# Dense products in two halves of 64 rows, the lower half one tile behind

## The chip, the core and the metric

The kernel runs on one core of one Trainium2 chip. The metric is the device time of one execution in microseconds (us). TensorE multiplies matrices into PSUM, VectorE, ScalarE and GpSimd work on vectors, and SyncE, ScalarE and GpSimd issue transfers (DMAs). TensorE has one queue of instructions; a matmul in it is preceded by the load of its stationary operand (its weights). PSUM has eight banks of 512 columns.

## The reference

Attention with a compressive memory beside a gated feed-forward block, mixed by a gate. Cut to what matters:

```python
for s in range(N):                                   # 4 chunks of L = 512 rows, 32 heads of 20
    logits = einsum("bhqd,bhkd->bhqk", qs, ks) * scale + mask
    a_dot = einsum("bhqk,bhkd->bhqd", softmax(logits), vs)
    num = einsum("bhld,bhde->bhle", phi(qs), M)
    den = einsum("bhld,bhd->bhl", phi(qs), z)[..., None] + 1e-6
    outs.append(g * num / den + (1.0 - g) * a_dot)
    M, z = M + einsum("bhld,bhle->bhde", phi(ks), vs), z + phi(ks).sum(2)
a = concat(outs) @ wo                                # D = 640
b = (silu(x @ w1) * (x @ w3)) @ w2                   # F = 1728
out = sigmoid((x * gate_w).sum(-1)) * a + (1 - that) * b
```

## The kernel before, in words

Everything dense (q, k, v, the two up products g and u, the down product f, the output product op) is a product of 640 or 128 rows at a time, in three passes of high and low parts in single precision's fast form. A **tile** is one PSUM bank: 15 matmuls of 128 rows by 512 columns for q, k, g and u, 15 of 320 columns for v and op, and 9 (in one group 5) of 320 columns for f. After its last matmul an engine empties the bank: VectorE and ScalarE make `ft`, `fu`, `ht` from g and u, VectorE adds f and op into `acc`.

The attention works on **pairs** of heads `p`, two pairs to a **quad**. A head has 60 or 62 rows, so the two heads of a pair stand in rows 0 to 63 and 64 to 127, and the array is split into two halves of 64 rows for them. For each pair there are three `s_unit`s (logits of queries against keys; VectorE takes each row's maximum, line 626, with an instruction that reads the maximum out behind each) and three `t_unit`s (the logits once more, turned, with the maximum taken off; ScalarE makes the exponential `P`, GpSimd cuts it at the diagonal). `pv_quad` multiplies P by V with the array cut into four column strips, 16 matmuls (32 on the chip, since plain single precision takes two passes).

TensorE's order is written by the program itself; the other engines' order comes from a scheduler. The attention is a generator of 40 slots for each quad. In four of them, `VISITS` (slots 5, 15, 25, 35), it issues its units together, s and t units of 1408 columns per head, the first with `pv_quad` ahead. Between visits the dense work is drawn from `segs`, a queue of jobs, by a credit in nanoseconds. Before a visit the running tile is carried up to the next place where its bank is filled. `bank_tile` hands out the eight banks in turn.

Weights are loaded by `w_load` into `wraw`, and split into high and low parts by `w_split` into one of `NW` = 6 buffers; `clock["oldest"]` says which weights are still needed.

Of the kernel before, what the change touches and what calls it, by code (L numbers as in the profile page):

```python
# [17 lines left out]
P = 128  # L18
# [8 lines left out]
NST, NW, NRAW, NHT, NVG, NB = 4, 6, 2, 6, 2, 8  # L27
# [6 lines left out]
PSEG = ((0, 512), (512, 384), (1024, 256), (896, 128))  # L34


@with_exitstack
def gated_mix(ctx: ExitStack, tc: tile.TileContext, xT, wqk, wv, w13, w2, w2h, wo, beta, out):
# [19 lines left out]
    sel = cp.tile([96, D], BF, name="sel")  # L58
    rs = cp.tile([P, P], F32, name="rs")
    rp = cp.tile([P, 3, P], BF, name="rp")  # L60
    rR = cp.tile([96, L], BF, name="rR")
# [28 lines left out]
    def selection():  # L90

        here(nc.gpsimd.memset(sel, 1.0))
        nc.gpsimd.affine_select(sel[:32], sel[:32], pattern=[[1, D]], base=0, channel_multiplier=-DH,
                                compare_op=ALU.is_ge, fill=0.0)
        nc.gpsimd.affine_select(sel[:32], sel[:32], pattern=[[-1, D]], base=DH - 1, channel_multiplier=DH,
                                compare_op=ALU.is_ge, fill=0.0)
        for i in (32, 64):
            nc.gpsimd.tensor_copy(sel[i:i + 32], sel[:32])
# [19 lines left out]
    free, held = list(range(NB)), {}  # L118

    def bank_tile(name, hold=None):  # L120


        k = free.pop(0)
        ps = pp.tile([P, L], F32, tag=f"b{k}", name=name, bufs=1)
        if hold:
            held[k] = -hold
        else:
            free.append(k)
        return ps

    def filled():

        free.extend(held)
        held.clear()

    def split_psum(dst, src, name, pin=lambda ins: ins):

        hi = bank_tile(name)[:, :src.shape[-1]]
# [37 lines left out]
    def w_split():  # L176
        k, raw, n, _, after = raws.pop(0)
        w = sp.tile([P, 2, D + 2], FR, tag="W", name=f"W{k}", bufs=NW)
        tiles[k] = w
        split(w[:, :, :n], raw[:, :n], lo=nc.vector.tensor_sub if k < 7 else None, pin=behind(after))  # L180
# [17 lines left out]
    def w_get(i, oldest=None):  # L198
# [6 lines left out]
        clock["oldest"] = i if oldest is None else oldest  # L205
# [81 lines left out]
    def proj(ps, w, x):  # L287
        n = 0
        for kb in range(KB):
            for a, b in PASSES:  # L290
                nc.tensor.matmul(ps, w[:, a, kb * P:(kb + 1) * P], x[:, b, kb, :],  # L291
                                 start=n == 0, stop=n == 14)
                n += 1
            if kb < KB - 1:
                yield 699
        filled()
# [47 lines left out]

    def q_block(c, mb, i, alloc, oldest=None):
        ps = bank_tile(f"q{c}_{mb}", 1300)
        yield from proj(ps, w_get(i, oldest), Xs[c])
        if c:
            if mb == 0:
                big["q", c] = alloc(f"pq{c}")  # L350
        s = parts(f"qs{c}_{mb}", ps, big["q", c][:, mb * L:(mb + 1) * L] if c else None)
        store_parts(0, c, mb, s)
        yield 699

    def q_pair(c, i, j):

        ws = [w_get(i), w_get(j, i)]
        ps = [bank_tile(f"q{c}_{mb}") for mb in range(2)]
# [14 lines left out]
    def memory_read(c):  # L373
        pq = big.pop(("q", c))[:, :KB * L].rearrange("p (b n) -> p b n", b=KB)
        for qb in range(4):
            for hf in range(2):
                gm = f_tile(f"gm{c}_{qb}_{hf}")[:, :320]
                ps = bank_tile(f"nd{c}_{qb}_{hf}")
                nd = ps[:, :16 * VE].rearrange("p (h e) -> p h e", e=VE)
                todo = []  # L380
                for b in range(KB):
                    a0, a1 = HEADS[b]
                    u0, u1 = max(a0, 16 * hf), min(a1, 16 * hf + 15)
                    if u0 <= u1:
                        todo.append((b, a0, u0, u1))
                for n, (b, a0, u0, u1) in enumerate(todo):
                    nc.tensor.matmul(nd[:, u0 - 16 * hf:u1 - 16 * hf + 1, :],  # L387
                                     pq[:, b, qb * P:(qb + 1) * P],
                                     Ms[c - 1, b][:, u0 - a0:u1 - a0 + 1, :],
                                     start=n == 0, stop=n == len(todo) - 1, skip_group_check=True)  # L390
# [6 lines left out]
                store_later(gd[c][:, qb, 320 * hf:320 * hf + 320], gm, ("g", c, qb), n=2)  # L397
                yield 700

    def v_blocks(c, iv, end):  # L400
# [6 lines left out]
        wvt = [w_get(i, iv[0]) for i in iv]  # L407
        for lb in range(4):
            if keep:
                vv = V[:, lb]  # L410
            else:
                vv = ht_tile([P, H, VE], F32, f"vv{c}_{lb}")
                nc.gpsimd.memset(vv[:, :, DH:], 1.0)
            for hf in range(2):
                n0, n1 = (0, 320) if hf == 0 else (320, 642)
                ps = bank_tile(f"v{c}_{lb}_{hf}", 800)
                n = 0
                for kb in range(KB):
                    for a, b in PASSES:
                        nc.tensor.matmul(ps[:, :n1 - n0], x[:, a, kb, lb * P:(lb + 1) * P],  # L420
                                         wvt[kb][:, b, n0:n1], start=n == 0, stop=n == 14)
                        n += 1
                    if end and (lb, hf) == (3, 1):
# [635 lines left out]
```

## Time and profile before

| | |
|---|---|
| time, median of 3 (lowest to highest) | 1131.27 us (1130.45 to 1131.47) |
| profiled execution, first to last instruction (its own time is not listed apart) | 1129.4 us |
| TensorE busy, its matmuls | 1119.2 us (99%), 6952 |
| VectorE, GpSimd, ScalarE busy | 575.5 us, 545.1 us, 483.1 us |
| granted TensorE clock, mean | 0.998 |

The page's busy time of TensorE is the union of overlapping matmuls whose ends are modelled, so 99% does not say that the array streams without loss. In the timeline a line is a run of equal instructions: when the run begins, how long it lasts to the last one's end, engine, line, operation, output and inputs, count. The next run's start, not the first one's length, tells how long it kept the engine. PEld is the load of weights. In the groups, the two numbers behind the bar are busy time in us and the mean life of one in ns; behind the next bar stands the engine's idle time ahead of them.

### The profile page before, as it was taken

Reading aid. Unit: us, or ns where it says so; the run is one execution under the profiler, and the core shown is the slowest. Engines: PE = TensorE matmul, PEld = TensorE weight load, DVE = VectorE, ACT = ScalarE, POOL = GpSimd, SP = SyncE. Lnnn points to the kernel's source line nnn. Section 1 sums busy time; section 2 is a strip of 40 time slices with the busy share of each in tenths; the row PEclk is TensorE's granted clock in tenths of the full one; section 3 lists DMA queues with packets and bytes.
Section 4 is the critical chain, followed back from the end, with each engine's and each line's share of the span. In section 5 each row is a group of like instructions: output and inputs, shape, how many; then the busy total and the mean of one; then the engine's idle time right before and its main releaser. Section 6 shows DMA issues by size and latency. Waiting matters only on the chain.

```text
span 1129.4 us, 19596 instructions
## 1 busy us (share of the span) xinstructions
PE 1119.2 (99%) x6952; PEld 903.7 (80%) x6952; DVE 575.5 (51%) x1719; ACT 483.1 (43%) x988; POOL 545.1 (48%) x732
## 2 busy tenths in 40 slices
PE   9999999999999999999999999999999999999998
PEld 6988777877877888888977776788768778877988
DVE  6032564355655553565243667774546665651544
ACT  6255334544343242255355644535543444344040
POOL 5053356455455453455255446645764555465140
PEclk9999999999999999999999999999999999999999
DMA  8265753434344324435377864456643334342122
GB/s 313 95 233 204 234 128 93 97 88 114 77 113 104 96 65 120 140 83 179 107 244 247 266 214 134 101 135 166 174 120 106 91 95 110 88 133 76 48 59 94
DMA packets 85953, 152.01 MB, mean 135 GB/s; under 512 B 19936, under 2 KB 32992, under 8 KB 85856
## 3 DMA queue, kind: packets, MB, share of 16 engines
q1 hardware_dynamic: 55776, 94.48, 26.8%
q0 software_dynamic: 22880, 41.86, 15.4%
q10 hardware_dynamic: 7200, 14.42, 3.4%
q8 instruction: 55, 0.90, 0.3%
q14 instruction: 42, 0.34, 0.1%
HBM read 95.25 MB, written 54.53 MB: 133 GB/s over the span
## 4 chain that ended last, share of the span: by engine, by line
PE 93%; issue 2%; DMA 1%; DVE 1%; POOL 1%; ACT 1%; POOLq 0%; SPq 0%; ACTq 0%; DVEq 0%
PE g L291 17%; PE f L571 17%; PE u L291 16%; PE v L420 6%; PE o L670 6%; PE k L291 6%; PE q L291 6%; PE s L618 5%; PE op L813 4%; PE t L653 4%; PE pm L474 1%; PE nd L387 1%; PE q L366 1%; PE pkt L459 1%; PE gt L737 1%
## 5 line engine op out<-in xcount | busy, mean ns | idle before, releaser
L626 DVE CUSTOM_DVE_ANT_0 junk<-s,mask 128x128 bf16<-128x128 f32 (+3 forms) x512 | 251.1, 490 | 189.8 <-PE s L618 150.9
L116 POOL TENSOR_TENSOR W<-wr,W 128x640 fp32r<-128x640 f32 (+1 forms) x126 | 197.5, 1571 | 203.8 <-ACT W L115 160.7
L657 ACT ACTIVATE P<-t 128x384 f32<-128x384 f32 (+1 forms) x384 | 174.5, 533 | 165.2 <-PE t L653 164.2
L291 PE MATMUL g<-X,W 128*128 128x512 f32 x840 | 216.4, 401 | 0.0
L660 POOL TENSOR_SCALAR_AFFINE_SELECT P<-P 128x256 f32<-128x256 f32 (+1 forms) x192 | 94.2, 497 | 235.7 <-ACT P L657 235.2
L571 PE MATMUL f<-W,ht 128*128 128x320 f32 x1312 | 204.4, 313 | 1.0 <-ACT acc L577 0.7
L291 PE MATMUL u<-X,W 128*128 128x512 f32 x780 | 201.1, 401 | 0.0
L571 PEld LDWEIGHTS f<-W,ht 128*128 128x128 f32 x1312 | 194.3, 189 | 7.6 <-issue 3.3
L291 PEld LDWEIGHTS g<-X,W 128*128 128x128 f32 x840 | 153.5, 188 | 40.1 <-issue 5.7
L291 PEld LDWEIGHTS u<-X,W 128*128 128x128 f32 x780 | 143.1, 188 | 36.3 <-issue 3.8
L115 ACT CAST W<-wr 128x640 fp32r<-128x640 f32 (+1 forms) x131 | 94.2, 730 | 73.2 <-PE u L291 23.1
L642 POOL DMA_DIRECT2D qk<-mr x128 | 73.4, 576 | 49.4 <-DVE mr L637 40.2
L579 DVE SCALAR_TENSOR_TENSOR acc<-f,cgate,acc 128x320 f32<-128x320 f32 x128 | 69.5, 547 | 41.6 <-PE f L571 40.7
L116 POOL TENSOR_TENSOR ht<-ft,ht 128x512 fp32r<-128x512 f32 x52 | 67.2, 1292 | 46.3 <-ACT ht L115 46.1
L291 PE MATMUL k<-X,W 128*128 128x512 f32 x300 | 77.1, 403 | 0.0
L670 PE MATMUL o<-P,vg 128*32 128x512 f32 (+3 forms) x1024 | 75.7, 436 | 0.0
L813 PE MATMUL op<-W,oT 128*128 128x320 f32 x480 | 75.3, 313 | 0.0
L813 PEld LDWEIGHTS op<-W,oT 128*128 128x128 f32 x480 | 71.2, 189 | 2.5 <-issue 1.6
L420 PE MATMUL v<-W,X 128*128 128x320 f32 (+1 forms) x480 | 72.1, 311 | 0.6 <-DVE m L626 0.6
L420 PEld LDWEIGHTS v<-W,X 128*128 128x128 f32 x480 | 71.0, 189 | 1.5 <-PE q L291 1.0
L597 POOL DMA_DIRECT2D qk<-qkd x128 | 70.1, 552 | 0.0
L653 PE MATMUL t<-qk 62*128 62x256 f32 (+2 forms) x512 | 68.1, 338 | 0.6 <-DVE ns L141 0.3
(115 smaller groups left out, 1103.0 us busy)
## 6 DMA issues: line engine op xcount, KB each, us to landing
qk<-qkd POOLq DMA_DIRECT2D x128, 240.0 KB, 3.9
wr<-in_w_dram SPq DMA_DIRECT2D x80, 320.0 KB
qkd<-qs SPq DMA_DIRECT2D x20, 512.0 KB
qkd<-ks SPq DMA_DIRECT2D x20, 512.0 KB
od<-oq ACTq DMA_DIRECT2D x32, 256.0 KB
wr<-in_wo_dram SPq DMA_DIRECT2D x20, 320.0 KB
vg<-vd SPq DMA_DIRECT2D x16, 336.0 KB
xr<-in_xT_dram SPq DMA_DIRECT2D x20, 256.0 KB
```

Source lines behind the costliest of these rows:

```text
L115: pin(nc.scalar.copy(dst[:, 0], src))
L116: (lo or nc.gpsimd.tensor_sub)(dst[:, 1], src, dst[:, 0].bitcast(F32))
L291: nc.tensor.matmul(ps, w[:, a, kb * P:(kb + 1) * P], x[:, b, kb, :], start=n == 0, stop=n == 14)
L420: nc.tensor.matmul(ps[:, :n1 - n0], x[:, a, kb, lb * P:(lb + 1) * P], wvt[kb][:, b, n0:n1], start=n == 0, stop=n == 14)
L571: nc.tensor.matmul(ps[:, :320], a, b, start=n == 0, stop=n == len(ms) - 1)
L626: nc.vector.tensor_tensor_reduce(out=junk[:, :n], in0=ps[i][:, o:o + n], in1=mask[:, L - n:], scale=1.0, scalar=-3.0e38, op0=ALU.add, op1= ...
L642: after(4 + 9 * k, lambda d=dst, r=r: here(nc.gpsimd.dma_start(d, mr[r:r + 8])))
L653: nc.tensor.matmul(ps[i][:, o:o + L - q0], k[:, kb * P:(kb + 1) * P], q[:, q0:], start=kb != 2, stop=kb != 3, skip_group_check=True)
L657: last["exp"] = nc.scalar.activation(u["P"][:, i, o:o + n], ps[i][:, b:b + n], AF.Exp, scale=SCALE)
L660: nc.gpsimd.affine_select(d, d, pattern=[[0, 2], [0, n], [1, P]], base=0, channel_multiplier=-1, compare_op=ALU.is_ge, fill=0.0)
L670: nc.tensor.matmul(ps[32 * i:32 * i + 32, kb * P:], heads[2 * p + i]["v"][:, kb], pairs[p + i // 2]["P"][:, i % 2, o:o + n], start=kb == 0 ...
L813: nc.tensor.matmul(ps[:, :320], oT[0][:, qb % 2, a, kb * P:(kb + 1) * P], ws[kb][:, b, 320 * hf:320 * hf + 320], start=n == 0, stop=n == 14)
```

## The change

A dense product of 128 rows becomes two of 64 rows, in the upper and the lower half of the array, which add into the same bank. First all upper halves of a tile are issued, then all lower halves, and while a tile's lower halves run the next tile's upper halves do. `Work` is a tile, `under` the tile in the upper half, `behind_one` those that wait for the lower, `flight` the one in it. `put` keeps a clock for each half, and `step` issues for the half that is behind. The lower half of a tile begins when `APART` = 5 further upper matmuls have been issued, and behind a read by VectorE of one element of the bank (`seen`), which shows that the upper half is done.

The visits are gone: each s and t unit stands alone in a slot (`S_AT`, `T_AT`) amid dense products, which now have its shape. `pv_quad` moves to slot 2 of the quad after next's (from 5) and is what still changes the array's division. Transposes, the memory's products and the sums' spreading (`rr`, with a selection matrix rebuilt by GpSimd in the head) go in halves too. A bank is chosen by an expected time at which it comes free (`until`, `hold`). `NW` is 7, and side jobs are braided in by nanoseconds.

```diff
-NST, NW, NRAW, NHT, NVG, NB = 4, 6, 2, 6, 2, 8
+NST, NW, NRAW, NHT, NVG, NB = 4, 7, 2, 6, 2, 8
+COL, COL4, MIN_MM, APART = 0.4533, 1.667, 110, 5
...
-    def bank_tile(name, hold=None):
-        k = free.pop(0)
+    def bank_tile(name, hold=1500):
+        k = until.index(min(until))
+        until[k] = max(clocks) + hold
...
+    def halves(todo):
+        def half(f, r):
+            o, l, x, c = f() if callable(f) else f
+            return o, l[64 * r:64 * r + 64], x[64 * r:64 * r + 64], c, False
+        return tuple([lambda f=f, r=r: half(f, r) for f in todo] for r in range(2))
...
+    def one(r, w):
+        i, todo = w.at[r], w.todo[r]
+        o, l, x, c, turn = todo[i]() if callable(todo[i]) else todo[i]
+        if turn:
+            ins = nc.tensor.transpose(o, l, x)
+        else:
+            ins = nc.tensor.matmul(o, l, x, start=i == 0 and (r == 0 or not w.todo[0]),
+                             stop=i == len(todo) - 1 and (r == 1 or not w.todo[1]), skip_group_check=True)
+        if r == 0 and i == len(todo) - 1 and w.todo[1]:
+            nc.vector.tensor_copy(seen, w.ps[:1, :1])
+        dense["ns"] += put(r, c) / 2
...
+    def follow():
+        if flight[0] is None and behind_one and dense["n0"] >= behind_one[0].mark + APART:
+            flight[0] = w = behind_one.popleft()
...
-    def proj(ps, w, x):
-                nc.tensor.matmul(ps, w[:, a, kb * P:(kb + 1) * P], x[:, b, kb, :],
-                                 start=n == 0, stop=n == 14)
+    def proj(w, x):
+        def parts(ps):
+            return halves([(ps, w[:, a, kb * P:(kb + 1) * P], x[:, b, kb, :], L * COL) for kb in range(KB) for a, b in PASSES])
...
-        for i in (32, 64):
-            nc.gpsimd.tensor_copy(sel[i:i + 32], sel[:32])
+        for base, h0, n, f0, f1 in ((0, 0, R1H + 1, 0, R1B * P), (64, R1H, H - R1H, R1B * P, D)):
...
-    VISITS = {5: (((0, 0), (0, 1)), ((0, 0),)), 15: (((0, 2), (1, 0)), ((0, 1),)),
-              25: (((1, 1), (1, 2)), ((0, 2),)), 35: ((), ((1, 0), (1, 1), (1, 2)))}
+    S_AT = {3: (0, 0), 8: (0, 1), 11: (0, 2), 16: (1, 0), 19: (1, 1), 24: (1, 2)}
+    T_AT = {5: (0, 0), 13: (0, 1), 21: (0, 2), 27: (1, 0), 31: (1, 1), 35: (1, 2)}
```

On TensorE before, behind the quad `o12` in chunk 0's attention: the rest of a tile of g (chunk 0, hidden tile 7), the whole tile of u, six matmuls of the next g, then a visit (the second unit of the pairs 16 and 17, one unit t of pair 14), and g goes on. `X0` and `X1` are the chunks' inputs, `W35` and `W36` weights, `qk` the pairs' buffers; the last number in a name is the buffer's:

```order
L291 MATMUL g0_7_3441<-X0_102,W35_2924 128x512 x3
L291 MATMUL u0_7_3519<-X0_102,W36_3247 128x512 x15
L291 MATMUL g1_7_3544<-X1_104,W35_2924 128x512 x6
L618 MATMUL s16_2_0_3551<-qk0_86 128x512
L618 MATMUL s16_2_1_3552<-qk0_86 128x512
```

The same place on TensorE now, behind the same quad; each dense row is a half:

```order
L195 MATMUL g1_7_4947<-X1_105,W35_4082 128x512
L195 MATMUL g0_7_4832<-X0_103,W35_4082 128x512
L195 MATMUL g1_7_4947<-X1_105,W35_4082 128x512
L195 MATMUL g0_7_4832<-X0_103,W35_4082 128x512
L811 MATMUL s16_0_0_4976<-qk0_86 128x256
L811 MATMUL s16_0_1_4977<-qk0_86 128x256
L811 MATMUL s16_0_0_4976<-qk0_86 128x256
L811 MATMUL s16_0_1_4977<-qk0_86 128x256
L195 MATMUL g1_7_4947<-X1_105,W35_4082 128x512
L195 MATMUL g0_7_4832<-X0_103,W35_4082 128x512
```

Where a tile's 15 matmuls stood in a row, upper halves of g1 and lower halves of g0 now take turns, and the logits of a pair stand between two such rows.

On VectorE before, in the down product of chunk 0 (f0_6, hidden tiles 6 to 8): the maxima of a unit of pair 19 (`junk`, with `m` read out behind each), then the sums into `acc0`, one for each tile of f:

```order
L626 ISA junk_3832,m36_3639<-s19_0_1_3823,mask_85 128x128
L626 ISA m36_3639 128x1
L626 ISA junk_3834,m36_3639<-s19_0_1_3823,mask_85 128x256
L626 ISA m36_3639 128x1
L546 SCALAR_TENSOR_TENSOR ft1_8_3798<-fu1_8_3799,u1_8_3802 128x512
L579 SCALAR_TENSOR_TENSOR acc0_1930<-f0_6_0_0_3856,cgate_101,acc0_1930 128x320
L579 SCALAR_TENSOR_TENSOR acc0_1930<-f0_6_0_1_3872,cgate_101,acc0_1930 128x320
```

The same unit of pair 19 on VectorE now:

```order
L198 COPY seen_96<-f0_6_3_0_5522 1x1
L820 ISA junk_5552,m36_5212<-s19_0_0_5546,mask_85 128x128
L820 ISA m36_5212 128x1
L820 ISA junk_5554,m36_5212<-s19_0_0_5546,mask_85 128x256
L820 ISA m36_5212 128x1
L820 ISA junk_5556,m36_5212<-s19_0_1_5547,mask_85 128x128
L820 ISA m36_5212 128x1
L762 SCALAR_TENSOR_TENSOR acc0_2777<-f0_6_1_1_5437,cgate_102,acc0_2777 128x320
L820 ISA junk_5558,m36_5212<-s19_0_1_5547,mask_85 128x256
L820 ISA m36_5212 128x1
L198 COPY seen_96<-f0_6_3_1_5543 1x1
```

Each tile has a copy into `seen` behind its upper half and, four tiles later in the queue, its sum; here a copy stands behind a unit's four maxima, and a sum among them.

More of the change, by code (lines that the diff above doesn't have):

```diff
@@ L874, in gen @@
         def gen():
[L875 to L882 removed]
+            side = Side(b[1], every, skip)
+            yield side
+            yield from a[1]
+            side.on = False
             if rest:
```

686 lines of the change are left out of this document (403 added, 283 removed).

## The prediction

> **What bounds the kernel now.** I read the page's busy shares first, then the chain that ended last, then who makes TensorE wait, and last the timeline of TensorE, where the loss shows.
>
> ```profile
> PE 1119.2 (99%) x6952; PEld 903.7 (80%) x6952; DVE 575.5 (51%) x1719; ACT 483.1 (43%) x988; POOL 545.1 (48%) x732
> PE 93%; issue 2%; DMA 1%; DVE 1%; POOL 1%; ACT 1%; POOLq 0%; SPq 0%; ACTq 0%; DVEq 0%
> L291 PE MATMUL g<-X,W 128*128 128x512 f32 x840 | 216.4, 401 | 0.0
> L571 PE MATMUL f<-W,ht 128*128 128x320 f32 x1312 | 204.4, 313 | 1.0 <-ACT acc L577 0.7 <-POOL W L116 0.3
> ```
>
> TensorE is busy for 99% of the span and makes up 93% of the chain; no other engine is above 51%. The 401 and 313 ns are whole lives of overlapping matmuls, not their spacing. The spacing is read from the timeline of TensorE (start, length, what, count):
>
> ```profile
> 22.35 35.63 PE L420 MATMUL v<-W,X 128*128 128x320 f32 x240
> 57.81 2.48 PE L291 MATMUL k<-X,W 128*128 128x512 f32 x10
> ...
> 220.68 1.55 PE L291 MATMUL u<-X,W 128*128 128x512 f32 x6
> 222.16 2.36 PE L670 MATMUL o<-P,vg 128*32 128x512 f32 x32
> 224.45 0.68 PE L618 MATMUL s<-qk 60*128 60x256 f32 x6
> 224.97 0.39 PE L653 MATMUL t<-qk 62*128 62x512 f32 x2
> 225.29 2.36 PE L291 MATMUL u<-X,W 128*128 128x512 f32 x9
> 227.49 2.26 PE L291 MATMUL g<-X,W 128*128 128x512 f32 x9
> 229.68 0.74 PE L618 MATMUL s<-qk 60*128 60x512 f32 x6
> 230.25 0.35 PE L653 MATMUL t<-qk 62*128 62x384 f32 x2
> 230.53 1.67 PE L291 MATMUL g<-X,W 128*128 128x512 f32 x6
> 232.03 3.63 PE L291 MATMUL u<-X,W 128*128 128x512 f32 x15
> 235.50 1.55 PE L291 MATMUL g<-X,W 128*128 128x512 f32 x6
> ```
>
> 240 products of 320 (or 322) columns take 57.81 - 22.35 = 35.46 us, 0.148 each; the 15 of 512 columns that begin at 232.03 take 3.47, 0.231 each: 0.451 ns per column. A logit visit costs more than its columns. At 229.68 four pairs stand (512, 256, 256 and 384 columns per head, both heads at once): 1408 columns, 0.635 us, but the next g starts 0.85 later. The 9 matmuls ahead take 2.19 where 9 x 0.231 is 2.08, the 6 behind take 1.50 where 1.39 would do. Together 0.22 + 0.11 + 0.11 = 0.44 us are lost where the array goes from 128 rows to two times 64 and back. Beyond its first microseconds TensorE waits for nobody:
>
> ```profile
> PE f L571 <- ACT acc L577: 0.7, 1, 0.7
> PEld o L670 <- issue: 37.6, 149, 0.4
> PEld s L618 <- issue: 21.8, 80, 0.4
> ```
>
> Its largest such wait for another engine is 0.7 us; what precedes o and s is put down to nothing that the profile shows, and that is the change of mode.
>
> **The change, part by part.** The sum is made against the profiled execution, whose span of 1129.4 us lies 1.9 below the median of 1131.27.
>
> *Switches removed.* There are four visits per four heads; by the loop that makes them, 100 hold only logits and 32 P times V. Dense products now have the logits' shape, so the 100 lose nothing any more: 100 x 0.44 = 44 us. A visit with P times V: 1.48 - 1.39 ahead of it, 2.29 for o itself, 0.84 - 0.635 among the logits, 2.20 - 2.08 behind, 2.70 in all. Alone, o keeps its entry, itself and its exit, 2.50; the 31 with logits save 0.20 each, 6.4 us. Removed: 50.4 us.
>
> *Twice as many matmuls, of half the rows.* 4,462 dense matmuls become 8,924 and as many loads. If the halves run side by side, each pair of halves takes what the whole took, 0 us. The logits already do so:
>
> ```profile
> 224.45 0.42 PEld L618 LDWEIGHTS s<-qk 60*128 60x128 f32 x6 [0.20 <-issue]
> 224.79 0.19 PEld L653 LDWEIGHTS t<-qk 62*128 62x128 f32 x2
> L618 PEld LDWEIGHTS s<-qk 60*128 60x128 f32 x512 | 38.6, 185 | 28.4 <-issue 21.8 <-DVE ft L546 1.5 <-DVE fu L540 1.1
> ```
>
> Two loads of t lie within 0.19 us where a single one of s lives 185 ns: the halves load together. From 224.45 to 224.97, six loads and six matmuls (256, 256 and 384 columns per head) take 0.52 us; the columns are 0.404, so one load of about 0.11 shows and two hide. At 229.68 it is the same: 0.57 for 0.462 of columns, one load of three. A stretch of 320-column halves needs four instructions in 0.148; this one issued twelve in 0.52 (0.043 each against 0.037), and o 64 in 2.29 (0.036). It is near that pace that the evidence ends. For and against: the rivals.
>
> The Trainium skill (TensorE: Matmul & The Clock Gate, Part 3, The mechanism) says that a weight load overlaps a running matmul only where the row group differs. By it each half would wait for its own load behind its own matmul, the sum would be some 490 us higher, and the trace, which hides two loads of three behind the same rows' matmul, disagrees.
>
> *The lower half trails.* In the order its first tile starts when the upper one has 20 matmuls behind it (15 of one tile, 5 of the next), and the upper one is done as much earlier: 20 x 0.231 = 4.6 us added.
>
> *A read by VectorE in every tile.* 439 copies of one element (line 198) stand between the upper half's last matmul and the lower half's first: the first lower matmul waits for the copy, and in TensorE's one queue every matmul behind it, of both halves. No such copy is in the trace; the nearest rows bound it at 83 to 171 ns, and I take 153, the row of one element per partition:
>
> ```profile
> L626 DVE CUSTOM_DVE_ANT_0 junk<-s,mask 128x512 bf16<-128x512 f32 x128 | 88.4, 691 | 41.0 <-PE s L618 29.0
> L626 DVE CUSTOM_DVE_ANT_0 junk<-s,mask 128x384 bf16<-128x384 f32 x128 | 71.2, 557 | 29.7 <-PE s L618 18.6 <-DVE m L626 0.5
> L579 DVE SCALAR_TENSOR_TENSOR acc<-f,cgate,acc 128x320 f32<-128x320 f32 x128 | 69.5, 547 | 41.6 <-PE f L571 40.7
> L626 DVE CUSTOM_DVE_ANT_0 junk<-s,mask 128x256 bf16<-128x256 f32 x128 | 54.2, 424 | 4.0
> L626 DVE DVE_READ_ACCUMULATOR2_ANT m<- 128x1 f32 x512 | 42.6, 83 | 0.1
> L626 DVE CUSTOM_DVE_ANT_0 junk<-s,mask 128x128 bf16<-128x128 f32 x128 | 37.2, 291 | 115.1 <-PE s L618 103.3
> L392 DVE SCALAR_TENSOR_TENSOR nd_r<-nd,gH 128x16 f32<-128x16 f32 x24 | 4.1, 171 | 5.5 <-PE nd L387 5.3
> L88 DVE TENSOR_SCALAR cR<-cR 128x1 f32<-128x1 f32 x1 | 0.2, 153 | 0.0
> 1113.26 11.62 PE L571 MATMUL f<-W,ht 128*128 128x320 f32 x77 [0.28 <-POOL W L116]
> 1124.91 0.55 DVE L579 SCALAR_TENSOR_TENSOR acc<-f,cgate,acc 128x320 f32<-128x320 f32 x1 [0.19 <-PE f L571]
> ```
>
> As work they are 439 x 0.153 = 67 us on an engine that idles for 550: nothing. As a wait: VectorE starts 0.03 after a matmul's end (1113.26 + 11.62 = 1124.88, then 1124.91). Of a 512-column tile the copy is through 0.401 + 0.03 + 0.153 = 0.58 us after the last upper matmul begins, say 0.62 with the way back; the lower half is due after five to six upper matmuls, 1.16 to 1.39. So 0.5 to 0.8 us are to spare, unless VectorE is in a unit's maxima: two heads of (291 + 83 + 424 + 83) are 1.76 us, of 557 + 83 1.28, of 691 + 83 1.55. In the order 60 of the 146 copies of 512-column tiles stand right behind such a unit. Where its pair comes right at the tile's end, the copy is about 0.8 late (0.47 to the pair's end, 1.4 of maxima, 0.2 for copy and ways, against 1.3). From 0 to 60 x 0.8 = 48 us; I take a quarter, 12 us, since a unit can stand anywhere in the 3.5 us of a tile. The 160 f tiles have no such trouble: their lower half follows some 3 us behind.
>
> *Banks.* That lag costs PSUM. An f tile held its bank for 9 x 0.148 + 0.31 + 0.03 + 0.55 = 2.2 us; now upper half, lag and lower half make 1.3 + 3.7 (25 f matmuls of each half between, in the order) + 1.3 + 0.9 = 7.2. With logits between, a tile comes each 1.6 us: 4.5 banks instead of 1.4, and the logits take some 1.5 more (24 tiles of 1.5 us in 24 us). Of 8 banks about 2 stay free, and 1.6 are taken per us, so each take has about 1.2 us in hand on average instead of over 3. How late a bank is freed the trace tells for f:
>
> ```profile
> DVE acc L579 <- PE f L571: 40.7, 67, 1.8
> ```
>
> 67 of 128 sums started as soon as TensorE was done; the other 61 stood behind other work of VectorE. The f stretches are 160 x 1.6 = 256 us with 410 takes. Between none late and 61 of 128 late by half a maximum (0.3), 0 to 59 us; I take one in five late by 0.2, 16 us. The Trainium skill (TensorEngine Tiling (Array Packing), Gotcha 1: PSUM Pressure) says that row tiling raises the pressure on PSUM; no run here shows yet by how much.
>
> *P times V* now comes 7 slots behind the last t instead of 10; between nothing and 32 x 0.5, I take 2 us. The larger selection matrix is built by GpSimd in the head, where it idles for 26.6 us ahead of 57.11:
>
> ```profile
> 27.48 0.71 POOL L93 TENSOR_SCALAR_AFFINE_SELECT sel<-sel 32x640 bf16<-32x640 bf16 x1
> ...
> 57.11 3.09 POOL L116 TENSOR_TENSOR W<-wr,W 128x640 fp32r<-128x640 f32 x2 [26.60 <-issue]
> ```
>
> Nothing there; without that cover its four selects of 1200 and 780 columns would cost (1200 + 780) x 2 x 0.71 / 640 = 4.4 us.
>
> *Sum:* -50.4 + 4.6 + 12 + 16 + 2 = -15.8; a span of 1113.6 and, with the 1.9, a time of 1115.5 us.
>
> **The rivals.** (a) *All new waits are covered.* 12 and 16 fall away: 1087.5 us. For it: today VectorE idles half the time. Against it: 60 copies behind maxima. 0.12.
> (b) *The copy becomes the gate (slower).* If each of the 60 pays its 0.8, TensorE stops for 48 instead of 12 us: 1151.5. From 0.46 us per such copy on (12 + 15.8 over 60) nothing is gained. For it: VectorE is in order, and a late copy stops both halves. Against it: 0.5 to 0.8 to spare. 0.19.
> (c) *The halves' loads stand in line.* Then 320-column pairs go at two loads, 0.22, instead of 0.148: 2,272 x 0.07 = 160 us, 1275 us. Against it: two loads of t in 0.19. 0.05.
> (d) *A load waits for its own half's matmul* (the rule above): 4,462 x 0.11 = 490 us, 1606 us. Against it: 0.52 us at 224.45. 0.02.
> (e) *Gain and waits cancel*: waits of 46 us or so instead of 30, within 0.2% of 1131.3 (2.3 us, about what a measurement of this kernel can tell). 0.09.
>
> **How the numbers follow.** My forecast (new waits of 5 to 43 us in all, 1090.5 to 1128.5) has 0.53. Faster: 0.53 + 0.12 = 0.65; the same 0.09; slower 0.19 + 0.05 + 0.02 = 0.26. The range goes from (a), 1087, to just above (b), 1152; out of it lie (c), (d), the upper part of (b) and a little below (a), 0.2 in all.
>
> **What would show it.** Right: 15 pairs of 512-column halves in 3.5 us in the timeline, logits amid without a gap, mode gaps at o alone, the copy at about 0.15 us, and TensorE's waits now named (VectorE's copy at g and u, banks at f, s and t) with 20 to 40 us in total. Wrong: pairs slower than 0.231 and 0.148 ((c), (d)); waits for the copy above 28 us ((b)); f stretches paced by VectorE, which would make the 16 the term that failed.

## The result and the profile after

| | before | after |
|---|---|---|
| time, median (lowest to highest) | 1131.24 us (1130.45 to 1131.47) | 1238.5 us (1236.33 to 1241.67) |
| ratio, 95% interval | | 1.0952 (1.0935 to 1.0968) |
| profiled span | 1129.4 us | 1234.4 us |
| mean granted TensorE clock | 0.998 | 0.970 |

The changed kernel is 107 us slower, far outside the range. The page of the kernel after: busy shares, the granted clock in 40 slices, the chain that ended last.

```profile
PE 1143.0 (93%) x11798; PEld 994.8 (81%) x11798; DVE 620.3 (50%) x2158; ACT 484.7 (39%) x988; POOL 551.4 (45%) x737
PEclk9989999999999999968989998998999899999999
PE 66%; DVE 11%; issue 8%; ACT 6%; DMA 5%; POOL 3%; SPq 1%; ACTq 0%; DVEq 0%; POOLq 0%
```

TensorE now stands idle for 1234.4 - 1143.0 = 91.4 us, where it was 1129.4 - 1119.2 = 10.2; it makes up 66% of the chain instead of 93%; and the clock has notches. It is not that halves are slow. In the timeline of the kernel after, 20 halves of 320 columns and the two of a logit pair go by without a gap:

```profile
300.63 0.48 PE L811 MATMUL s<-qk 60*128 60x512 f32 x2
300.86 1.73 PE L195 MATMUL f<-W,ht 64*128 64x320 f32 x20
302.36 0.46 PE L847 MATMUL t<-qk 62*128 62x512 f32 x2
302.59 1.70 PE L195 MATMUL f<-W,ht 64*128 64x320 f32 x20
```

From 300.86 to 302.36 ten pairs take 1.50 us, 0.150 a pair, and the logits 0.23 for 512 columns per head: no switch. Over the whole trace at full clock, the median of six pairs in a row is 0.886 us for 320 columns and 1.400 for 512, the same as six whole products before. What TensorE waits for is the new thing. The view of waits of the kernel after (engine, line, releaser: us in all, times, longest), its matmuls first, then its weight loads:

```profile
PE rr L195 <- DMA rR<-rp: 13.3, 3, 6.7
PE g L195 <- DVE seen L198: 11.5, 11, 3.9
PE pm L195 <- ACT pkn L634: 6.4, 3, 5.9
PE u L195 <- DVE seen L198: 5.8, 5, 2.7
PE pkt L193 <- DVE seen L198: 5.3, 1, 5.3
PE f L195 <- DVE acc L762: 4.2, 5, 1.3
PEld g L195 <- DVE seen L198: 17.7, 17, 4.3
PEld o L865 <- POOL P L855: 3.6, 7, 1.6
```

`seen` is the copy of line 198. Adding up, over all matmuls, how much later one starts than the one ahead and its columns allow (below, "stops"), 47.6 us in 56 stops end with that copy (the loads' rows of the view alone, all tiles together, have 44), 14.2 with the loads of rR, 11.6 with VectorE's sums (banks), some 30 with single products of ScalarE and VectorE that the next matmul reads (pkn, oT, gm, nd_r, pk, P). How one of them comes about, in the timeline of all engines:

```profile
463.32 0.72 ACT L124 CAST W<-wr 128x640 fp32r<-128x640 f32 x1 [2.26 <-DMA wr<-in_w_dram]
463.95 0.59 ACT L715 ACTIVATE ft<-g 128x512 f32<-128x512 f32 x1
464.65 0.69 DVE L716 SCALAR_TENSOR_TENSOR fu<-ft,g 128x512 f32<-128x512 f32 x1 [6.78 <-ACT ft L715]
465.25 0.55 DVE L820 CUSTOM_DVE_ANT_0 junk<-s,mask 128x384 bf16<-128x384 f32 x1
465.95 0.56 DVE L820 CUSTOM_DVE_ANT_0 junk<-s,mask 128x384 bf16<-128x384 f32 x1
466.44 0.14 DVE L198 COPY seen<-g 1x1 f32<-1x1 f32 x1
466.63 0.50 PE L195 MATMUL g<-X,W 64*128 64x512 f32 x1 [3.88 <-DVE seen L198]
```

A weight is late (2.26); ScalarE stands at its cast, with the tanh behind it; VectorE stands at the product that needs the tanh (6.78), with two maxima and the copy behind that; and TensorE stands 3.88 us for a copy of 0.14. Behind it the clock drops. The windows view of the kernel after (PE, PEld, DVE, ACT and POOL busy, then granted clock, DMA share, GB/s):

```profile
463.00:467.00 4.00, 0.37 (x4) 0.33 (x6) 2.12 (x7) 1.22 (x2) 1.54 (x1) 1.00 0.51 166
467.00:470.50 3.50, 3.50 (x22) 2.94 (x20) 1.57 (x5) 1.49 (x3) 1.49 (x2) 0.57 0.48 149
```

There are twelve such stretches, 76.3 us in all (7.4 before); the last one runs some 2 us past the kernel's end, here and before. Matmuls ran in 56 us of them, which costs about 28; before it was 2.

So the 105.0 us more of span are 81.2 more of standing idle, 26 more of half clock, and -2 for the rest. Without new losses that rest would be -50, the switches that went; so another 48 us of loss don't show as idle time. Some 20 of them belong to the stops named above, since idle time counts only from the modelled end of the matmul ahead: the stops are 103 us, the idle time rose by 81.2. What is left, over 20 us, would be stops too small to be counted, and was not taken apart.

### The profile page after: what moved, and what is told of

It is laid out like the page before. It is cut to its first block, busy times and chain, and to the rows that moved or that the text cites. A ratio compares the mean times of both kernels' runs of the same rounds, so it can differ in the third digit from the quotient of the medians.

```text
span 1234.4 us, 29973 instructions
## 1 busy us (share of the span) xinstructions
PE 1143.0 (93%) x11798; PEld 994.8 (81%) x11798; DVE 620.3 (50%) x2158; ACT 484.7 (39%) x988; POOL 551.4 (45%) x737
## 4 chain that ended last, share of the span: by engine, by line
PE 66%; DVE 11%; issue 8%; ACT 6%; DMA 5%; POOL 3%; SPq 1%; ACTq 0%; DVEq 0%; POOLq 0%
PE f L195 13%; PE g L195 13%; PE u L195 11%; PE o L865 5%; PE op L195 4%; PE v L195 4%; DVE junk L820 4%; PE q L195 4%; PE k L195 3%; PE t L847 3%; PE s L811 3%; POOL W L125 2%; ACT P L852 1%; DMA wr<-in_w_dram 1%; PE pm L195 1%
## 5 line engine op out<-in xcount | busy, mean ns | idle before, releaser
L195 PE MATMUL g<-X,W 64*128 64x512 f32 x1680 | 393.2, 401 | 11.6 <-DVE seen L198 11.5
L195 PE MATMUL u<-X,W 64*128 64x512 f32 x1560 | 379.9, 402 | 6.0 <-DVE seen L198 5.8
L195 PEld LDWEIGHTS g<-X,W 64*128 64x128 f32 x1680 | 270.6, 188 | 35.4 <-DVE seen L198 17.7
L195 PE MATMUL f<-W,ht 64*128 64x320 f32 x2624 | 280.4, 318 | 8.3 <-DVE acc L762 4.2
L195 PEld LDWEIGHTS u<-X,W 64*128 64x128 f32 x1560 | 259.5, 189 | 22.6 <-DVE seen L198 8.1
L195 PEld LDWEIGHTS f<-W,ht 64*128 64x128 f32 x2624 | 259.6, 192 | 15.6 <-DVE acc L762 7.0
L124 ACT CAST W<-wr 128x640 fp32r<-128x640 f32 (+1 forms) x131 | 93.6, 726 | 111.0 <-PE u L195 25.1
L195 PE MATMUL op<-W,oT 64*128 64x320 f32 x960 | 104.9, 312 | 6.2 <-ACT oT L124 3.4
L195 PE MATMUL k<-X,W 64*128 64x512 f32 x600 | 104.0, 411 | 0.6 <-DVE seen L198 0.6
L195 PEld LDWEIGHTS op<-W,oT 64*128 64x128 f32 x960 | 93.6, 185 | 10.9 <-ACT oT L124 5.2
L195 PE MATMUL q<-X,W 64*128 64x512 f32 x540 | 96.3, 402 | 5.2 <-DVE seen L198 5.1
L811 PE MATMUL s<-qk 60*128 60x256 f32 (+2 forms) x512 | 95.9, 330 | 2.9 <-DMA qk<-qkd 1.2
L125 POOL TENSOR_TENSOR ht<-ft,ht 128x512 fp32r<-128x512 f32 x52 | 67.2, 1292 | 47.9 <-ACT ht L124 47.6
```

Source lines behind the costliest of these rows:

```text
L125: (lo or nc.gpsimd.tensor_sub)(dst[:, 1], src, dst[:, 0].bitcast(F32))
L195: ins = nc.tensor.matmul(o, l, x, start=i == 0 and (r == 0 or not w.todo[0]), stop=i == len(todo) - 1 and (r == 1 or not w.todo[1]), skip_ ...
L811: nc.tensor.matmul(ps[i][:, o:o + n], q[:, qb * P:(qb + 1) * P], k[:, :n], start=qb != 1, stop=qb != 0, skip_group_check=True)
```

## The experiments

The theories, as they came up. H: TensorE stands at the copy, whose engine is in order and behind; H1, behind its own maxima, as the prediction argued; H2, because that engine itself waits. B: banks come free too late. M: the switches were cheap, so there was nothing to save. D and O: single transfers (the sums) or the new order in general put a consumer too close behind its producer. L: the halves make each tile last longer and tie TensorE to another engine, and that uses up the slack that every wait of the others had.

Each run was made beside runs of the kernel before. Idle is the span less TensorE's busy time, half clock the sum of the stretches at 0.5, the last one's 1 to 3 us behind the kernel's end included.

| run | us (lowest to highest) | ratio to before (95%) | idle | half clock |
|---|---|---|---|---|
| copy_scalar | 1228.9 (1226.6 to 1231.4) | 1.087 (1.085 to 1.089) | 90.7 | 70.9 |
| light_max | 1206.2 (1204.0 to 1212.8) | 1.068 (1.064 to 1.071) | 78.1 | 60.2 |
| light_max_before | 1125.8 (1125.7 to 1126.0) | 0.996 (0.994 to 0.997) | 7.3 | 2.9 |
| spread_before | 1210.1 (1209.1 to 1211.4) | 1.070 (1.069 to 1.072) | 8.4 | 3.1 |
| lag_3 | 1234.3 (1232.7 to 1236.5) | 1.091 (1.090 to 1.093) | 90.6 | 66.3 |
| lag_6 | 1243.7 (1241.8 to 1245.5) | 1.100 (1.098 to 1.101) | 93.6 | 96.1 |
| gate_product_later | 1236.8 (1236.4 to 1238.6) | 1.094 (1.092 to 1.095) | 94.7 | 72.8 |
| sums_later | 1228.8 (1224.9 to 1230.4) | 1.087 (1.085 to 1.089) | 83.1 | 74.1 |
| weights_earlier | 1221.4 (1220.6 to 1225.7) | 1.081 (1.079 to 1.083) | 86.5 | 52.1 |
| weights_and_sums | 1208.6 (1205.4 to 1211.0) | 1.068 (1.066 to 1.071) | 73.2 | 60.3 |
| weights_sums_lag_3 | 1208.8 (1207.3 to 1210.2) | 1.069 (1.067 to 1.070) | 77.3 | 45.5 |
| light_weights_sums | 1182.0 (1179.1 to 1184.5) | 1.045 (1.043 to 1.047) | 61.4 | 50.2 |
| two_banks_upper | 1219.7 (1215.7 to 1223.4) | 1.078 (1.076 to 1.081) | 83.9 | 76.5 |
| two_banks_sum | 1338.5 (1338.0 to 1339.7) | 1.184 (1.182 to 1.185) | 146.5 | 125.1 |
| two_banks_all | 1159.0 (1156.2 to 1160.5) | 1.025 (1.023 to 1.027) | 46.1 | 39.4 |
| whole_new_order | 1296.1 (1293.0 to 1300.5) | 1.147 (1.144 to 1.150) | 20.4 | 19.1 |

### Was there anything to save? The switch measured by itself

spread_before:

```diff
-    VISITS = {5: (((0, 0), (0, 1)), ((0, 0),)), 15: ...}
+    VISITS = {2: ((), ()), 3: (((0, 0),), ()), 5: ((), ((0, 0),)), 8: (((0, 1),), ()), ...}
```

> The kernel before, dense products in whole tiles of 128 rows, but with the logits' units one by one at the slots of the changed kernel: 192 visits with logits alone and 32 with P times V alone, instead of 100 and 32. By the prediction's prices (0.44 per visit of logits, 2.50 for P times V alone against 2.70 with logits) that adds 192 x 0.44 + 32 x 2.50 - 100 x 0.44 - 32 x 2.70 = 34 us: 1165 us. Theory M (a switch costs half of that or less, so that there was little to save): 1140 to 1150 us. Much above 1165 would say that spreading the units makes waits of its own, even without halves.

It took 79 us more than before, not 34, but the count in that expectation was wrong: there are 384 units, not 192. In its trace 318 visits hold only logits (some units stand side by side), and over them TensorE loses 0.437 us each beyond the columns, against 0.46 for the 100 of the kernel before: 46.1 and 139.1 us. With P times V that makes 91 us more, 79 measured (close visits share a matmul between them). Theory M falls. One such visit, in the timeline of that run:

```profile
238.63 1.67 PE L291 MATMUL g<-X,W 128*128 128x512 f32 x6
240.23 0.50 PE L618 MATMUL s<-qk 60*128 60x256 f32 x4
240.66 0.50 PE L291 MATMUL g<-X,W 128*128 128x512 f32 x1
```

Six products of 0.231 take 1.60 instead of 1.39, and two pairs of 256 columns 0.43 instead of 0.23. So the 50.4 us were there to be had.

### Whose queue is it? The copy and what stands ahead of it

copy_scalar:

```diff
-            nc.vector.tensor_copy(seen, w.ps[:1, :1])
+            nc.scalar.copy(seen, w.ps[:1, :1])
```

> The one-element copy between a tile's upper and lower half is made by ScalarE instead of VectorE; nothing else is changed. Theory H (the loss is TensorE standing at the copy because VectorE's queue, which is in order, is behind: 47.6 us of the stops over 0.45 us end with that copy, and stops of over 2.4 us are followed by 3.4 to 6.8 us at half clock): the stops change place with ScalarE's queue, which is 39% busy instead of 50% and also stands for weights; they fall to 15 to 30 us and the time to 1190 to 1215 us. Theory B (late banks are the loss): unchanged, 1233 to 1243 us, since a bank is freed by the same instructions. Theory M (the 50.4 us of switches were never to be had): unchanged too.

9.6 us faster, less than the 23 to 48 expected: 46.5 us of stops end with the copy again, only that they stand elsewhere. The waits of that run:

```profile
PE u L195 <- ACT seen L198: 13.2, 7, 6.1
PE pm L195 <- ACT seen L198: 6.3, 1, 6.3
ACT W L124 <- DMA wr<-in_w_dram: 26.7, 9, 6.1
```

ScalarE is busy for 43% of that run, and the copy is as late there. In 45.5 us that TensorE stood at the copy (stops over 0.1 us), ScalarE split weights for 12.7 us, stood for weights for 7.2 and did or awaited other things for the rest. It is not VectorE's load that matters so much as that any in-order queue has work and waits of its own in it.

light_max and its control:

```diff
-                nc.vector.tensor_tensor_reduce(out=junk[:, :n], in0=ps[i][:, o:o + n], in1=mask[:, L - n:],
-                                               scale=1.0, scalar=-3.0e38, ...
+                nc.vector.tensor_tensor_reduce(out=junk[:, :32], in0=ps[i][:, o + n - 32:o + n], in1=mask[:, L - 32:],
+                                               scale=1.0, scalar=100.0, ...
```

> The row maxima read only 32 columns of each block and start from a constant of 100, so the maxima are left out of the computation; their instructions stay in number and order, but one takes about 0.15 us instead of 0.29 to 0.69. Theory H1 (VectorE's own maxima ahead of the copy, as the prediction argued): the copy's stops fall from 47.6 to under 15 us, with them most half-clock stretches, time 1165 to 1190 us. Theory H2 (what is ahead of the copy is mostly VectorE itself waiting for ScalarE, a weight or a DMA): 30 us or more of the stops stay, 1205 to 1225 us. Theory B: the 11.6 us of stops for VectorE's sums go, about 1220 us, and the copy's stops stay.

> The same light maxima in the kernel before, as a control (maxima left out of the computation). TensorE waited for VectorE nearly nowhere there, so every theory expects 1128 to 1132 us. A larger gain would say that maxima cost time even without the copy.

32 us faster in halves, 5 in whole tiles: 27 us go to the maxima. The copy's stops fall from 47.6 to 33.6 only, so H1, the mechanism of the prediction, is a part, and most of the copy's stops have another cause. H2 is a part as well, and not the rest. Laid beside VectorE's rows, 45.9 us of the kernel after in which TensorE stood at a copy (stops over 0.1 us) hold 12 us of maxima, 3 of copies, 20 of VectorE's other work (the turning of the maxima, `mr`, 4.4, X 2.7, ht 2.5, oT 1.8 the largest) and 11 in which VectorE itself stood, 4.2 of them for ScalarE's phi_t and 2.2 for its ft. Work can of course be late because of a wait further ahead. The control came out 5 us faster, where none to 3 were expected: its visits lose 0.42 instead of 0.46.

gate_product_later:

```diff
-                    nc.vector.scalar_tensor_tensor(u, t, 1.0, pg, op0=ALU.add, op1=ALU.mult)
+                    later.append((dense["ns"] + FU, lambda: nc.vector.scalar_tensor_tensor(u, t, 1.0, pg, ...)))
...
-            name, evac, hold = (("g", evac_gate(c), 1600), ("u", evac_up(c), 900))[k]
+            name, evac, hold = (("g", evac_gate(c), 2600), ("u", evac_up(c), 900))[k]
```

`FU` is 1400.

> VectorE's gate product u = (t + 1) x g (line 716), which waits for ScalarE's tanh, is put into VectorE's queue 1.4 us of dense work later, so that VectorE need not stand in it with copies behind. Theory H2 (VectorE itself waits for ScalarE ahead of the copies: 53.4 us in 30 waits of that line): 10 to 25 us of the copy's stops go and some half-clock stretches with them, 1205 to 1225 us. Theory H1 (VectorE's maxima are what is ahead) or B: 1234 to 1245 us, since g's bank is held 1.4 us longer.

This one tells nothing: the scheduler put the product back to nearly the same place in VectorE's queue (at 466.54 us it stands between the copies of u and g as it did at 464.65), and its waits are the same, 52.4 us in 30 after 53.4 in 30:

```profile
DVE fu L720 <- ACT ft L719: 52.4, 30, 10.2
```

weights_earlier (NRAW, the raw weight buffers):

```diff
-NST, NW, NRAW, NHT, NVG, NB = 4, 7, 2, 6, 2, 8
+NST, NW, NRAW, NHT, NVG, NB = 4, 7, 3, 6, 2, 8
```

> Three raw weight buffers instead of two, so a weight's load is issued one weight earlier; nothing else. Theory H2 (VectorE stands for ScalarE, which stands for a weight's load, 24.5 us in 10 waits, and the copy stands behind): the stops at 463, 512, 528 and 624 us go, 12 to 25 us faster with their half-clock stretches, 1213 to 1226 us. If late weights are themselves only the consequence of TensorE's stops: 1233 to 1240 us.

17 us faster, as H2 expected. The time that TensorE stood at a copy falls from 45.9 to 37.5 us, VectorE's own standing in it from 11 to 4; the other gain is half clock, in which matmuls ran 38 us instead of 56. ScalarE's waits for these weights, in the kernel after and in this run:

```profile
ACT W L124 <- DMA wr<-in_w_dram: 24.5, 10, 5.0
```

```profile
ACT W L124 <- DMA wr<-in_w_dram: 7.5, 4, 2.6
```

In the kernel before the same row reads 18.4 us in 12 waits, and TensorE hardly felt them (its longest wait beyond the head was 0.7 us):

```profile
ACT W L115 <- DMA wr<-in_w_dram: 18.4, 12, 6.1
```

### How far behind? The lag

lag_3, and lag_6 with a 6 for the 3 (and with the wait for the sums, `while qb not in ready`, of sums_later below):

```diff
-        if flight[0] is None and behind_one and dense["n0"] >= behind_one[0].mark + APART:
+        if flight[0] is None and behind_one and dense["n0"] >= behind_one[0].mark + (3 if behind_one[0].name[0] in "gukq" else APART):
```

> In the 512-column tiles (g, u, k, q) the lower half may start 3 upper matmuls behind the end of its upper half instead of 5: 2 x 0.231 = 0.46 us less for the copy to be made in; banks are held as much shorter. Theory H (the copy is late because its engine's in-order queue is busy or itself waiting): the copies that are late now lose 0.46 more each, and many that are just in time become late: 60 to 100 of 146, +28 to +46 us, 1265 to 1285 us. Theory B (banks): 2 to 8 us faster, 1230 to 1236 us.

> The same lag at 6 instead of 5, the most that the order of this kernel takes: 0.231 us more for the copy. Theory H: the 56 counted stops and as many smaller ones get 0.231 shorter, 15 to 25 us, part of it lost to banks held longer: 1215 to 1230 us. If only few, very long waits make the loss (VectorE standing several us for ScalarE or a weight), 0.23 us of lag changes little: 1233 to 1238 us. Theory B: 1240 to 1250 us.

Neither theory had the signs. With 3 the copy's stops rose from 47.6 to 72.5 us, much as H said, yet the time fell by 4; with 6 they fell to 37.7, and the time rose by 5. The other stops went the opposite way. With 3, those for VectorE's sums fell from 11.6 to 2.1, for pkn from 7.6 to 1.7, for oT from 8.6 to 3.6, in all by 20 to 26 us, by how small a stop is counted. With 6, those for rR, P and pkn rose by some 17. All starts over 0.45 us late, whatever they wait for, come to 109 or 110 us with each of the three lags. What differs is the half clock: matmuls ran 50 us in it with 3, 56 with 5 and 70 with 6, and half the differences, 3 less and 7 more, is about what the time did. A tile in halves is done later by its lag, and whatever takes a bank or reads a result soon after pays for it. TensorE's idle time, 90.6 and 93.6 for 91.4, hardly moves. Taking the read away altogether wasn't tried: the halves would write one bank with nothing to order them. A lag above 6 wasn't either.

### The new order: sums, and halves against whole tiles

sums_later:

```diff
-        turned.append(c)
+        after(10, turned.append, c)
...
+                    while qb not in ready:
+                        dense["n0"] += 20
+                        step(None)
```

> The spreading of the reciprocal sums (rr) joins the order 10 steps later than its six loads (line 911) are queued instead of at once. Theory D (these loads are late, behind a weight's load in SyncE's queue: 14.2 us of stops in 3, two of 6 to 7 us, each with a half-clock stretch behind it of about 2 us of loss): 15 to 19 us faster, 1219 to 1224 us. If the stop only moves to the next thing that needs these sums (the output products): 1233 to 1240 us.

9.7 us faster, between the two expectations; the stops for rR fell from 14.2 to 5.6 us. Their cause stands in the lines of rR, of the kernel before and after (issues by SyncE; ns from shortest over median to longest, first and last start):

```profile
L713 SPq DMA_DIRECT2D rR<-rp x12: 547/610/692, 371.5 to 1056.1; - x12
```

```profile
L911 SPq DMA_DIRECT2D rR<-rp x24: 771/817/847, 386.8 to 1155.0; - x24
```

A chunk's sums are now six loads of 0.82 us each on SyncE, 4.9, instead of three of 0.61, 1.8, and rr is in the order right behind them.

weights_and_sums makes both edits:

> Three raw weight buffers and the spreading of the sums 10 steps later. If each stop has a cause of its own, the two gains add: 10 us from the sums and that of the weights, 1205 to 1218 us. If the time is set by one coupled chain that only moves from wait to wait, the sum of both is less than the larger alone: 1224 to 1232 us.

29.9 us faster, where 17.1 and 9.7 make 26.8: the gains add.

whole_new_order keeps the changed kernel's order and planner, but a product is one tile of 128 rows again (and banks are given out by another rule, by which a pair's two tiles of logits never take the same one):

```diff
-        return tuple([lambda f=f, r=r: half(f, r) for f in todo] for r in range(2))
+        return [lambda f=f: (*(f() if callable(f) else f), False) for f in todo], []
```

> The changed kernel's order and planner (single pairs of logits, its waits put where the planner puts them), but every dense product in whole tiles of 128 rows: no halves, no lag, no copy between halves (the transposes stay in halves). The switches come back: the kernel before with its logits spread took 1210 us with 318 visits at 0.437. Theory O (the new order puts consumers too close behind producers, weights and sums too late): TensorE stands idle 45 us or more beside the switches, 1250 to 1275 us. Theory L (the halves' longer tiles, 8.2 us from the first matmul to the last instead of 3.5, and the copy between them use up the slack that this order and the 8 banks have): idle under 20 us as in the kernel before with its logits spread (8.4), 1195 to 1220 us.

Slower than either theory's time, because there are 386 visits with logits alone (0.47 us each, 181 us) and the transposes, still in halves, switch too. But what tells the theories apart is the idle time: 20.4 us, not 91, and 7 of these for rR. ScalarE's waits for weights are as long as ever, and TensorE doesn't feel them (the page's busy shares, then the view of waits):

```profile
PE 1270.5 (98%) x7072; PEld 908.1 (70%) x7072; DVE 580.7 (45%) x1749; ACT 486.6 (38%) x988; POOL 551.3 (43%) x737
```

```profile
ACT W L124 <- DMA wr<-in_w_dram: 24.0, 11, 4.8
PE rr L230 <- DMA rR<-rp: 6.6, 2, 6.0
```

That is theory L: the halves, not the order, turn other engines' waits into TensorE's. Two reservations: this run is 58 us longer, which gives every producer more time, and it has another rule for banks and the wait for the sums of sums_later.

### Do the causes add up, and what is left?

light_weights_sums puts light_max, weights_earlier and sums_later together; weights_sums_lag_3 adds the lag of 3 to weights_and_sums.

> Light maxima (left out of the computation), three raw weight buffers and the later sums, all three in halves as changed. If their causes are separate, the gains add (27 net of the control, 30 for weights and sums): 1175 to 1185 us, idle 45 to 55 us. If one chain only moves from wait to wait: 1195 to 1206 us. In both it stays above 1131, so the rest of the loss lies elsewhere: lag, the copy behind other work, banks.

> Weights and sums as in that run of 1208.6 us, with a lag of 3 in the 512-column tiles. Alone, a lag of 3 raised the copy's stops by 25 us and lowered the others by 29 (VectorE's sums, pm, pk, output products). Theory L (both ends of the lag cost alike, so it is at its best place between): 1203 to 1210 us. If with the weights early VectorE is no longer late for the copies: 1190 to 1200 us.

1182.0, inside the range of separate causes. Alone, light_max gained 32.3 us and the other two 29.9, in sum 62.2; together they gain 56.5. So these causes are separate but for some 6 us. (The 27 net of the control is what the maxima cost because of the halves; in this sum the whole 32.3 counts.) TensorE still stood 19.8 us at copies, 17 of them with VectorE at work, little of it maxima. The lag of 3 gives nothing (1208.8), as L says of a cost with two ends.

two_banks_upper takes the tie between the halves away. Each half has a bank, the copy stands behind both, the lower half's product is left out of what follows, and banks are given out as in whole_new_order, with the wait for the sums of sums_later:

```diff
+            w.ps2 = pp.tile([P, L], F32, tag=f"b{k}", name=w.name + "_l", bufs=1)
+            w.todo = w.todo[0], w.parts(w.ps2)[1]
...
-        if r == 0 and i == len(todo) - 1 and w.todo[1]:
+        if r == 0 and i == len(todo) - 1 and w.todo[1] and w.ps2 is None:
             nc.vector.tensor_copy(seen, w.ps[:1, :1])
...
+            nc.vector.tensor_copy(seen, w.ps2[:1, :1])
         w.evac(w.ps)
```

> Each dense tile gets two banks, one for each half; the halves run abreast and nothing stands between them. VectorE still reads one element, but of the finished lower half, with no matmul of that tile behind it. The lower half's product is left out of what follows. Theory H (the tie between the halves, that is the copy, its engine's queue and the lag it forces, makes the loss): the switches' saving shows, 1090 to 1135 us. Theory O (the new order itself puts consumers too close behind their producers: rr, pm, nd, output products, about 45 us of stops with their half-clock stretches): 1170 to 1200 us. Theory B (banks): two banks for 3.5 us each in place of one for 8 changes little, 1215 to 1240 us.

two_banks_sum adds the lower half in place of the last line added:

```diff
-            nc.vector.tensor_copy(seen, w.ps2[:1, :1])
+            low = sp.tile([P, L], F32, tag="low", name="low", bufs=1)[:, :w.width]
+            nc.scalar.copy(low, w.ps2[:, :w.width])
+            nc.vector.tensor_add(w.ps[:, :w.width], w.ps[:, :w.width], low)
```

> The same with nothing left out: ScalarE copies the finished lower half to memory (about 0.59 us for 512 columns) and VectorE adds it to the upper (0.69), for some 380 tiles: about 190 us more on ScalarE (485 now) and 220 on VectorE (620 less 60 of copies). Theory H, if these two engines keep up: 1105 to 1150 us. If VectorE, at about 780 of 1150 us and in order, frees banks too late: 1180 to 1240 us. Theory O: 1180 us or more.

two_banks_upper is 18.8 us faster only, inside theory B's range (1215 to 1240) and above H's and O's. Part of the stops moved to the logits, which now wait for a bank until VectorE has read it. Some of its waits, loads first (its profiled execution, 1223.37 us, was the longest of four and had a granted clock of 0.95 for most of its first 970 us, which no other trace here shows):

```profile
PEld t L909 <- DVE seen L235: 10.6, 17, 1.6
PEld s L873 <- DVE seen L235: 4.8, 7, 1.3
PE rr L245 <- DMA rR<-rp: 11.7, 3, 6.2
```

With the lower halves really added, VectorE works 791.6 us instead of 620.3, and the time is 1338.5: 98 us above the range of the theory in which VectorE frees banks too late, so the price of that work was put far too low (theory O, 1180 or more, had no upper end and is not tested).

two_banks_all joins two_banks_upper with the three edits above:

> Light maxima, earlier weights and later sums (1182.0 us so far), and with them two banks per dense tile, so that no copy stands between the halves and they need no lag; the maxima and the lower half's product are left out of what follows. Theory L (what is left is the tie between the halves: the copy and the lag): the rest of the waits go too, 1115 to 1145 us. Theory B (PSUM: a tile's two banks for half as long are as scarce as one for 8 us): s and t wait for banks instead, 1165 to 1190 us.

1159.0, below B's range and above L's: of what was left, 23 us go with the tie, in a run that also leaves the lower half's product out and has its own rule for banks. In its quiet stretches nothing stops any more (the windows view, TensorE's matmuls and loads first; the granted clock stands before the DMA share):

```profile
850.00:900.00 50.00, 50.00 (x578) 44.32 (x577) 22.19 (x123) 20.39 (x42) 25.32 (x36) 1.00 0.45 119
```

28 us above the kernel before stay, with idle 46.1 and half clock 39.4: single stops for rR, oT, banks of s and t, loads of the logits, each with its half clock behind it. These were not taken apart further.

## Why the prediction was wrong, by its own steps

The sum had 34.6 us of new losses against 50.4 of gain. With that gain really made, the 105.0 us more of span hold 155 us of new losses: 47.6 of stops at the copy, 14.2 for rR, 11.6 for VectorE's sums, some 30 for other single products, 26 of half clock, and some 26 that were not taken apart.

- **Switches removed, -50.4: right.** Measured 0.46 over 100 visits and 0.437 over 318.
- **Halves side by side, 0: right.** 0.148 to 0.150 per pair of 320 columns; (c) and (d) are false.
- **The lower half trails, 4.6**: not measured apart. But its real price is another: each result comes later, and lag_3 showed 20 to 26 us of other stops that hang on 0.46 us of it.
- **The copy, 12 (0 to 48): this is the step that failed.** Its stops are 47.6 us. That this is (b)'s number is chance, since (b) had it from maxima alone, and stops are not all it costs. The step asked what could stand ahead of the copy in VectorE's queue, and found only maxima. They are 12 of the 46 us laid beside VectorE's rows above; 20 are VectorE's other work, and 11 are what VectorE *waits* for with the copy behind. The step put both at nothing. The waits were in the profile before, 49.0 us at the gate product alone, and harmless, since TensorE read VectorE's results much later:

```profile
DVE fu L540 <- ACT ft L539: 49.0, 22, 6.4
```

  With a copy in each tile, a part of them is TensorE's. Of the time, 27 us go with the maxima (light_max against its control), 17 with the late weights (weights_earlier), 23 with the tie itself (two_banks_all against light_weights_sums, with the reservation made there). VectorE's other work ahead of the copy was read from the trace; no run took it away by itself.
- **Banks, 16 (0 to 59)**: the direct stops, 11.6 for VectorE's sums, are of that size. That banks are scarce is shown by two_banks_upper, where waits went to s and t when no copy stood between the halves. The Trainium skill (TensorEngine Tiling (Array Packing), Gotcha 1: PSUM Pressure) says that row tiling raises the pressure on PSUM, and here the runs agree: 11.6 us of stops for VectorE's sums, where before no wait of TensorE for a sum was above 0.7.
- **P times V, 2: right** in size: 3.6 us of waits for GpSimd's P, 1.1 before (the loads' rows).
- **Selection matrix, 0**: no wait of TensorE for the matrix shows, but the step stopped at it. The same lines double the loads of rR, and those cost 13.3 us of waits and 9.7 of time when moved. Each of a moved step's transfers was to be counted.
- **The clock: not in the sum at all.** 26 us, as a consequence of the stops.

No rival held: (b) came out at the copy's stops by chance and ended at 1151.5, because it priced only copies late behind maxima and left the other terms of the sum as they were. f was not paced by VectorE.

## What to carry to other kernels

A handshake put into an engine's stream, however short the instruction, makes that engine wait for all that the other one does or waits for ahead of it: before pricing it, read that engine's whole queue, its *waits* as well as its work, and not its busy share. And a change that lengthens the life of each tile is to be priced at what takes its bank or reads its result next: a shorter lag moved stops to the handshake, a longer one to the readers. When several causes add up (27, 17, 10 and 23 here) no single fix brings the gain back.

## What the hardware showed

Stops of TensorE cost more than their length. Nine of the twelve half-clock stretches of the kernel after followed an idle gap of 1.8 us or more, and all but the one cut off by the end last 3.41 us or a multiple (6.83 mostly, once 17.07): a gap of 2.66 us at 524.9 and the clock at 0.5 from 528.9, 5.31 at 621.1 and from 624.5. The Trainium skill (TensorE: Matmul & The Clock Gate, Part 1, What's actually happening) gives a free-running window of 3413 ns for this, and the lengths agree.

The Trainium skill's rule (TensorE: Matmul & The Clock Gate, Part 1, HAM oscillation) is to leave no idle gap above some 3.4 us; here gaps of 1.98 us at 508.7 and of 2.66 us were followed by half clock, while one of 2.21 at 712.3 was not. The trace shows why: all twelve stretches begin on one grid of 3.413 us. Cut along that grid, the 1.98 us lie in one window, and the 2.21 are split into 0.9 and 1.3. In this trace all ten windows at full clock with 1.75 us idle or more were followed by half clock. Of those with 1.2 to 1.61 us one was, at the very end, and the rest were not; one of 1.18 us in many small gaps was. In lag_6 some windows with 1.26 us idle and more were followed too. So it is the idle share of a window that counts here, about half of it or less, and not a single gap; the exact rule stays open.
